# Banded attention woven into a four-block feed-forward: token copies, the pace of the attention pairs, and the order of a few steps

## The chip, the cores and the metric

The kernel runs on 1 core of one Trainium2 chip. The time is device microseconds of one execution. Two executions of the kernel before gave 535.16 and 535.59 us, a median of 535.38 us; the execution that was profiled took 535.26 us.

## The reference

An attention with a banded mask feeds a bilinear feed-forward:

```
scores = q @ k^T / 8 + bias(head, key distance)    # 4 batches, 8 heads, 768 tokens, 64 per head
keep   = key < 8  or  0 <= query - key < 96
x      = softmax(scores where kept) @ v            # as a 3072 x 512 matrix of tokens
out    = ((x @ w1) * (x @ w2)) @ w3 @ w_out        # 512 -> 1024 -> 1024 -> 512, all float32
```

Since at most 104 keys are kept for a query, the kernel computes scores only in bands of 136 columns.

## The kernel before, in words

**Attention.** The 3072 tokens are 24 blocks `s` of 128 queries; two blocks make a pair `d` (0 to 11) of 256 tokens. A block goes through `scores` (L762, TensorE), `maxima` (L776, VectorE adds the bias and takes the row maximum, per quarter `q` and head half), `exponentials` (L785, ScalarE), `sums` (L792), `scale_part` (L809) and `turn` (L814), the last three on VectorE: they normalise and transpose the weights. When both blocks of a pair are turned, `values` (L822, TensorE) multiplies with `v` in 192 small matmuls, the first 64 of which need only the pair's first block, and `tokens` (L902) copies the result out of PSUM on ScalarE. One PSUM tile `sc` holds scores and values in turn.

**Feed-forward.** Tokens are taken in units `u`: unit 1 holds pairs 2 and 3 and multiplies plainly ("U", `first`, L278: half a product is six 512-column matmuls). Units 2 and 3 hold four blocks of 256 tokens each and use the seven-product scheme of fast matrix multiplication (`Sevenths`): for each of eight chunks `f` of the 1024 hidden columns come products p = 1, 5, 4 (of the chunk before), 6, 2, 3 (of the chunk before), 7, each of six matmuls, accumulated in two PSUM tiles `x` and `y`. After each, `take` (L400) works on the sums: p = 1, 6, 5 are copied by ScalarE (L410), p = 2, 7, 4, 3 are added or multiplied by VectorE (L412 to L419). p = 1 opens a tile (`room`, L394) in a ring of three buffers, tag `ag`, which output tiles also use. Unit 4 (`Wide`, L432) does the same on 512-token blocks made from pairs 8 to 11. "Z" items (`third`, L312) are the second multiplication, three 512-column matmuls with the folded matrix `w3 @ w_out`, eight for each 128 tokens.

**Operands.** All operands are split in a high and a low part (ScalarE copies, VectorE subtracts). The weights `w12h` and `w12l` hold eight chunks; while unit 1 multiplies, VectorE and ScalarE form sums of weight blocks (`join` L201, `combine` L209, `sums_high`, `sums_low`) and write them out to DRAM; `bring` (L243) loads them back into the first seven eighths of the same buffers for units 2 to 4. The last eighth then is free. The tokens of pairs 8 and 9 wait there: `wide_tokens` (L858) copies them from PSUM into a tile of the `ag` ring, and two DMAs per pair move them on (L866). Later `first_tokens` and `first_low` (L939, L949) split them, and `next_tokens` (L957) makes the other operands of unit 4 in seven steps, placed at the Z items of unit 3 that `WIDE_AT` (L57) names.

**Order.** Until pair 4 the order is written out (`ORDER`). From there `planned` (L997) lists the feed-forward's items, and a loop places attention steps between them: `on(k)` (L1105) emits the next k items, `rows` (L1108) emits the quarters of a block with the given number of items after each, `rest` (L1116) emits `sums`, `scale_part` and `turn` in one or two parts, with an item between parts. Per pair `MEET` (L59) has the item before which `values` stands, the one before which the next pair's `scores` stand, and the paces of its two blocks: SLOW is two items after each quarter, QUICK is 1, 2, 1, 2. Every engine runs its instructions in that order, and DMAs are issued from SP in that order too. For pairs 4 and 5 the loop has its own paces.

Of the kernel before, what the change touches and what calls it, by code (L numbers as in the profile page):

```python
# [20 lines left out]
P = 128  # L21
# [70 lines left out]
class FeedForward:  # L92
# [3 lines left out]
    def __init__(self, ctx, tc, w12, w3k, w3t, w_out, out):  # L96
        self.nc = tc.nc
        self.w12, self.w3k, self.w3t, self.w_out, self.out = w12, w3k, w3t, w_out, out
        self.wp = wp = ctx.enter_context(tc.tile_pool(name="wp", bufs=1))
        self.mp = ctx.enter_context(tc.tile_pool(name="mp", bufs=2))  # L100
        self.ps = ctx.enter_context(tc.tile_pool(name="ps_m", bufs=4, space=PSUM))
        self.w = [wp.tile([P, NFC, 2, NCC, P], F32R, name=f"w12{x}") for x in "hl"]
        self.wh, self.wl = wp.tile([P, NFC, DO], F32R, name="wh"), [None] * NFC
        self.places, self.free, self.raw = list(range(NFC)), [NFC], {}

        self.wo = self.mp.tile([P, NFC, DO], I32, tag="gh", bufs=1, name="wo")
        gl = self.mp.tile([P, 2, 4 * PC], I32, tag="gl", bufs=1, name="stage")
# [4 lines left out]
        self.wf = [w.rearrange("p f n i m -> p (f n i m)") for w in self.w]  # L112

# [80 lines left out]
    def high(self, f):  # L194
        self.nc.scalar.activation(self.w[0][:, f].rearrange("p n i m -> p (n i m)"), self.t3s[:, f % 2].bitcast(F32), AF.Copy)

    def low(self, f):
        hi, lo = (w[:, f].rearrange("p n i m -> p (n i m)") for w in self.w)
        self.nc.vector.tensor_tensor(out=lo, in0=self.t3s[:, f % 2].bitcast(F32), in1=hi.bitcast(F32), op=ALU.subtract)

    def join(self, f):  # L201

        if f == 0:
            self.sums = self.xp.tile([P, 2, 4, 2 * P], F32, tag="xh", name="block_sums")
            self.parts = self.xp.tile([P, 2, 4, 2 * P], F32R, tag="xl", name="block_parts")
        hi, lo = (w[:, f].rearrange("p n i m -> p (n i m)").bitcast(F32) for w in self.w)
        self.nc.vector.tensor_tensor(out=self.sums[:, f % 2].rearrange("p k m -> p (k m)"), in0=hi, in1=lo, op=ALU.add)
# [19 lines left out]
    def blocks_out(self, f):  # L227
        for h in range(2):
            x = self.w[h][:, f].bitcast(F32).rearrange("p n (k i) m -> p n k (i m)", k=2)
# [3 lines left out]
    def restore(self):  # L233
        for f in range(NFC):
            for h in range(2):
                x = self.w[h][:, f].bitcast(F32).rearrange("p n (k i) m -> p n k (i m)", k=2)
                self.nc.sync.dma_start(out=x[:, 0], in_=self.ws[f, :, 0:2, h])
                self.nc.sync.dma_start(out=x[:, 1], in_=self.ws[f, :, 3:6:2, h])
# [30 lines left out]
class Unit:  # L269
# [8 lines left out]
    def first(self, f, n, half):  # L278

        if half == 0:  # L280
            self.ps[f, n] = self.ff.ps.tile([P, self.width], F32, tag="m", name=f"m_{self.c}_{f}_{n}")
        ps, (xh, xl) = self.ps[f, n], self.x
        for i in range(half * NCC // 2, (half + 1) * NCC // 2):
            mh, ml = (w[:, f, n, i] for w in self.ff.w)
# [78 lines left out]
class Sevenths(Unit):  # L363
# [36 lines left out]
    def take(self, p, f):  # L400
# [6 lines left out]
        y, z = (self.bank(k, f)[0] if p != 1 else None for k in (5, 2))  # L407
# [231 lines left out]
def banded(ctx, tc, ff, ns, nt, n1, nf, oki, qk, vx, sc, pr):  # L639
# [218 lines left out]
    def wide_tokens(d):  # L858

        x = d % 2 * T  # L860
        if d // 2 == LAST:
            raw = ff.mp.tile([P, NCC, T], F32, tag="ag", bufs=3, name=f"tokens_{d}")
            nc.scalar.activation(raw, sc[:, :, :T], AF.Copy)
            for k in range(2):
                to = ff.wf[k][:, 2 * SLOT:].bitcast(F32).rearrange("p (i t) -> p i t", i=2)
                nc.sync.dma_start(out=to[:, :, x:x + T], in_=raw[:, 2 * k:2 * k + 2])  # L866
            return
# [6 lines left out]
        b11, b21 = (ff.wf[k][:, 2 * SLOT:] for k in range(2))  # L874
# [12 lines left out]
        def hi(to, x):  # L887
            return lambda: nc.scalar.activation(to, x, AF.Copy)

        later[LAST] = [  # L890
# [5 lines left out]
            [sub(b11, b22, b22h)],  # L896
            [sub(b21, raw, t4h)],
        ]
        view = dict(b11=(a[:, :n], a[:, n:]), b21=(b[:, :n], b[:, n:]), t1=(t1h, t1l), t2=(t2h, t2l), t3=(t3h, t3l), t4=(t4h, b21), b22=(b22h, b11))
# [39 lines left out]
    def first_tokens(u, k=0):  # L939

        if u == LAST:
            if k == 0:
                homes[u] = [xp.tile([P, 2048], F32R, tag="xh", name=f"xh{i}_{u}") for i in range(2)]
            nc.scalar.activation(homes[u][k][:, :1024], ff.wf[k][:, 2 * SLOT:].bitcast(F32), AF.Copy)
            return
        homes[u] = [xp.tile([P, 2048], F32R, tag=tag, name=f"{tag}0_{u}") for tag in ("xh", "xl")]
        nc.scalar.activation(homes[u][0][:, :1024], ff.tokens[:, 0], AF.Copy)

    def first_low(u, k=0):  # L949

        if u == LAST:
            x = homes[u][k]
            nc.vector.tensor_tensor(out=x[:, 1024:], in0=ff.wf[k][:, 2 * SLOT:].bitcast(F32), in1=x[:, :1024].bitcast(F32), op=ALU.subtract)
# [21 lines left out]
    units, homes, later = {}, {}, {}  # L975
# [21 lines left out]
    def planned():  # L997
# [43 lines left out]
        for u in range(1, last + 1):  # L1041
# [11 lines left out]
            for t in range((2 if u < last else 4) * T // P):  # L1053
                for j, f in enumerate(line(u)):
# [23 lines left out]
                    if t == 3 and 0 <= j < 5 and u < last:  # L1078
                        yield seventh(u + 1, 0, (1, 5, 6, 2, 7)[j])

    with tc.manual_schedule(engines={mybir.EngineType.PE}):
        with tc.manual_schedule(engines={mybir.EngineType.DVE, mybir.EngineType.SP, mybir.EngineType.Activation, mybir.EngineType.Pool}):
            ordered()
        with tc.manual_schedule(engines={mybir.EngineType.Activation, mybir.EngineType.DVE}):
# [42 lines left out]
            for d in range(STEPS // 2, PAIRED):  # L1127
# [16 lines left out]
            for d in range(PAIRED, n // 2):  # L1144
# [3 lines left out]
                for s in (2 * d, 2 * d + 1):  # L1148
                    rows(s, MEET[d][2 + s % 2])
                    if s % 2 == 0:  # L1150
# [4 lines left out]
                    on(1)  # L1155
                    rest(s, 2)
# [51 lines left out]
```

## Time and profile before

| | |
|---|---|
| profiled execution | 535.26 us, span of its instructions 533.5 us |
| TensorE (PE) busy | 507.2 us, 95% of the span |
| VectorE (DVE) busy | 348.3 us, 65% |
| ScalarE (ACT) busy | 228.1 us, 43% |
| mean granted TensorE clock | 0.984 of full |

PE is busy nearly throughout, so the span is its work plus the places in which it waits, plus what it does at a lower clock. A row of a timeline has the start, the length, the engine, the line, the operation with the tiles it writes and reads, and in brackets how long the engine had been idle before it, with what ended the idle time. A matmul's length contains its pipeline latency: the next one starts before it ends.

### The profile page before, as it was taken

Reading aid. Unit: us, or ns where it says so; the run is one execution under the profiler, and the core shown is the slowest. Engines: PE = TensorE matmul, PEld = TensorE weight load, DVE = VectorE, ACT = ScalarE, POOL = GpSimd, SP = SyncE. Lnnn points to the kernel's source line nnn. Section 1 sums busy time; section 2 is a strip of 40 time slices with the busy share of each in tenths; the row PEclk is TensorE's granted clock in tenths of the full one; section 3 lists DMA queues with packets and bytes.
Section 4 is the critical chain, followed back from the end, with each engine's and each line's share of the span. In section 5 each row is a group of like instructions: output and inputs, shape, how many; then the busy total and the mean of one; then the engine's idle time right before and its main releaser. Section 6 shows DMA issues by size and latency. Waiting matters only on the chain. (4 is left out here: it accounts for less than half of the span.)

```text
span 533.5 us, 13891 instructions
## 1 busy us (share of the span) xinstructions
PE 507.2 (95%) x5812; PEld 409.0 (77%) x5812; DVE 348.3 (65%) x878; ACT 228.1 (43%) x662; POOL 4.0 (1%) x29
## 2 busy tenths in 40 slices
PE   7999999999999599998999999699989999999997
PEld 5445478888888488888998878699868888887885
DVE  7999888998988916677686575386773333336110
ACT  7157856354453323554545454455533121222220
POOL 2000000000000000000000000000000000000000
PEclk9999999999999889999999999799989999999999
DMA  8998629993699966378914266781011573100111
GB/s 317 418 342 340 268 81 304 363 355 105 211 318 307 301 218 212 127 238 271 346 65 119 88 236 214 260 283 62 2 40 62 162 215 117 38 1 6 54 41 63
DMA packets 40087, 100.97 MB, mean 189 GB/s; under 512 B 3538, under 2 KB 22994, under 8 KB 38482
## 3 DMA queue, kind: packets, MB, share of 16 engines
q1 hardware_dynamic: 39872, 99.76, 54.3%
q8 instruction: 47, 0.77, 0.6%
q10 hardware_dynamic: 146, 0.26, 0.1%
q14 instruction: 22, 0.18, 0.1%
HBM read 75.89 MB, written 23.07 MB: 186 GB/s over the span
## 5 line engine op out<-in xcount | busy, mean ns | idle before, releaser
L790 ACT ACTIVATE pr<-pr,mx 128x136 f32<-128x136 f32 (+2 forms) x192 | 74.8, 392 | 41.5 <-DVE mx L783 41.4
L410 ACT ACTIVATE ag<-x 128x256 f32<-128x256 f32 (+1 forms) x48 | 21.7, 452 | 79.2 <-PE x L385 70.6
L318 PE MATMUL o<-wh,gh 128*128 128x512 f32 x128 | 51.5, 402 | 0.1
L285 PE MATMUL m<-xh,w12h 128*128 128x512 f32 x128 | 50.2, 392 | 0.0
L319 PE MATMUL o<-wl,gh 128*128 128x512 f32 x128 | 50.1, 392 | 0.0
L320 PE MATMUL o<-wh,gl 128*128 128x512 f32 x128 | 50.1, 391 | 0.0
L286 PE MATMUL m<-xl,w12h 128*128 128x512 f32 x128 | 49.8, 389 | 0.0
L287 PE MATMUL m<-xh,w12l 128*128 128x512 f32 x128 | 49.8, 389 | 0.0
L834 PE MATMUL sc<-pt,vr 32*64 32x160 f32 (+4 forms) x2112 | 35.7, 279 | 8.6 <-DVE pt L820 8.6
L834 PEld LDWEIGHTS sc<-pt,vr 32*64 32x64 f32 x2112 | 32.9, 138 | 14.3 <-DVE pt L820 10.5
L385 PE MATMUL x<-xh,w12h 128*128 128x256 f32 (+1 forms) x152 | 34.9, 309 | 6.9 <-ACT ag L410 5.2
L820 DVE STREAM_TRANSPOSE pt<-pr 128x640 f32<-128x640 f32 (+1 forms) x36 | 37.5, 1055 | 2.1 <-ACT pr L805 1.8
L790 ACT ACTIVATION_READ_ACCUMULATOR pr<-pr,mx 128x1 f32 x192 | 36.4, 189 | 0.0
L783 DVE CUSTOM_DVE_ANT_0 pr<-sc,biasw 128x136 f32<-128x136 f32 x144 | 34.3, 294 | 2.1 <-PE sc L774 1.9
L385 PE MATMUL x<-xh,w12l 128*128 128x256 f32 (+1 forms) x152 | 34.1, 304 | 1.3 <-ACT ag L410 0.7
L385 PEld LDWEIGHTS x<-xh,w12h 128*128 128x128 f32 x152 | 26.9, 195 | 9.4 <-ACT ag L410 5.6
L336 ACT ACTIVATE ot<-o 128x512 f32<-128x512 f32 x23 | 13.6, 593 | 39.1 <-PE o L320 39.0
L252 PE MATMUL w<-wo,kt 128*128 128x512 f32 x64 | 28.5, 599 | 1.8 <-DVE wo L188 1.1
L385 PE MATMUL x<-xl,w12h 128*128 128x256 f32 (+1 forms) x96 | 29.6, 322 | 0.0
L385 PE MATMUL x<-xl,w12l 128*128 128x256 f32 (+1 forms) x96 | 29.2, 318 | 0.0
L385 PEld LDWEIGHTS x<-xh,w12l 128*128 128x128 f32 x152 | 26.2, 190 | 3.8 <-ACT ag L410 1.2
L318 PEld LDWEIGHTS o<-wh,gh 128*128 128x128 f32 x128 | 24.3, 190 | 5.9 <-issue 1.3
(195 smaller groups left out, 1066.2 us busy)
## 6 DMA issues: line engine op xcount, KB each, us to landing
qr<-qk SPq DMA_DIRECT2D x20, 720.0 KB, 6.9
w12h<-ws SPq DMA_DIRECT2D x16, 512.0 KB, 4.8
w12l<-ws SPq DMA_DIRECT2D x16, 512.0 KB, 5.1
vr<-vx SPq DMA_DIRECT2D x8, 768.0 KB, 6.3
w12h<-ws SPq DMA_DIRECT2D x8, 768.0 KB, 5.7
w12l<-ws SPq DMA_DIRECT2D x8, 768.0 KB, 6.1
out_dram<-ot SPq DMA_DIRECT2D x23, 256.0 KB, 2.1
raws<-w SPq DMA_DIRECT2D x5, 1024.0 KB, 6.0
```

The lines of the kernel that those rows point to most:

```text
L252: self.nc.tensor.matmul(self.prod[f], lhsT=block.bitcast(F32), rhs=self.wo[:, k].bitcast(F32), start=k == 0, stop=k == NFC - 1)
L285: self.nc.tensor.matmul(ps, lhsT=mh, rhs=xh[:, i], start=i == 0, stop=False)
L286: self.nc.tensor.matmul(ps, lhsT=mh, rhs=xl[:, i], start=False, stop=False)
L287: self.nc.tensor.matmul(ps, lhsT=ml, rhs=xh[:, i], start=False, stop=i == NCC - 1)
L318: self.nc.tensor.matmul(ps, lhsT=gh, rhs=ff.wh[:, f], start=f == first, stop=False)
L319: self.nc.tensor.matmul(ps, lhsT=gh, rhs=ff.wl[f], start=False, stop=False)
L320: self.nc.tensor.matmul(ps, lhsT=gl, rhs=ff.wh[:, f], start=False, stop=f == last)
L385: self.nc.tensor.matmul(out, lhsT=w[:, i], rhs=x[:, i], start=fresh and i == 0 and j == 0, stop=i == 1 and j == 2, skip_group_check=True)
L783: nc.vector.tensor_tensor_reduce(out=pr[:, q, u, GLB + w0:GLB + w1], in0=scored(s, u, q, w0, w1), in1=bias, scale=-SCALE, scalar=3.0e38, o ...
L790: nc.scalar.activation(x, x, AF.Exp, bias=mx[:, q, u:u + 1], scale=-1.0, accum_out=sm[:, q, u:u + 1])
L820: nc.vector.transpose(strided(pts[d][:, (half * NR + q0) * 2 * PF:], [PF, 2 * (q1 - q0)], [P, NR + 1], [1, R]), x.rearrange("p n (k c) -> ...
L834: nc.tensor.matmul(sc[cols, hp, n0 * R:n1 * R], lhsT=v[rows, i, cols], rhs=turned, start=i == i0, stop=i == NV - 1, skip_group_check=True)
```

## The change

- **Copies.** The eighth chunk of the weights gets two buffers of its own (`tail0`, `tail1`). Pairs 8 and 9 are copied by ScalarE straight from PSUM into them, in two instructions of 128x512 instead of one of 128x1024; the `ag` tile and the four DMAs are gone. The low parts of two operands of unit 4 are later written into the same buffers.
- **Pair 4.** Its second block has one item after each quarter instead of two, and no four items behind them; its first block is scaled and turned in halves. Its `values` stand after 19 items of unit 1 instead of 21.
- **Pairs 6 to 11.** The items before which `values` stand (24, 53, 80, 105, 134, 161) become 28, 58, 86, 112, 142, 169: four items more for pair 6, one more for each of pairs 7 to 10, none for pair 11. Behind the last `turn` of a pair, `values` follow after 3, 2, 2, 2, 2 and 1 items, where it was 1 for all. In pairs 7 to 11 the second block's `scores`, and in pairs 6 to 10 the load of later keys, move from before the first block's `sums` to between its `scale_part` and `turn`, three items later.
- **Unit 4.** The seven steps stand four to seven Z items later; its first products come in the order 1, 2, 5, 6, 7; in its last chunks, the split of chunks 4 to 6 stands after product 4 of the last chunk instead of product 3 of the one before.

```diff
-SPLITS = {(7, 6): (0, 4), (6, 3): (4, 7), (7, 3): (7, 8)}
-WIDE_AT = (1, 5), (1, 6), (1, 7), (2, 1), (2, 2), (2, 4), (2, 6)
+SPLITS = {(7, 6): (0, 4), (7, 4): (4, 7), (7, 3): (7, 8)}
+WIDE_AT = (2, 4), (2, 5), (2, 6), (2, 7), (3, 0), (3, 1), (3, 2)
-MEET = {6: (24, 27, QUICK, SLOW), 7: (53, 56, SLOW, SLOW), 8: (80, 83, SLOW, QUICK), 9: (105, 108, QUICK, QUICK), 10: (134, 137, SLOW, SLOW), 11: (161, 0, SLOW, QUICK)}
+MEET = {6: (28, 31, SLOW, SLOW), 7: (58, 61, SLOW, SLOW), 8: (86, 89, SLOW, QUICK), 9: (112, 115, QUICK, QUICK), 10: (142, 145, SLOW, SLOW), 11: (169, 0, SLOW, QUICK)}
...
-        self.w = [wp.tile([P, NFC, 2, NCC, P], F32R, name=f"w12{x}") for x in "hl"]
+        self.w = [wp.tile([P, NFC - 1, 2, NCC, P], F32R, name=f"w12{x}") for x in "hl"]
+        self.ends = self.last_blocks()
...
+    def tail(self, k, name, dtype):
+        return self.wp.tile([P, 2 * NCC * P], dtype, tag=f"tail{k}", name=f"{name}{k}")
...
         if d // 2 == LAST:
-            raw = ff.mp.tile([P, NCC, T], F32, tag="ag", bufs=3, name=f"tokens_{d}")
-            nc.scalar.activation(raw, sc[:, :, :T], AF.Copy)
+            if d % 2 == 0:
+                raws.extend(ff.tail(k, "raw", F32) for k in range(2))
             for k in range(2):
-                to = ff.wf[k][:, 2 * SLOT:].bitcast(F32).rearrange("p (i t) -> p i t", i=2)
-                nc.sync.dma_start(out=to[:, :, x:x + T], in_=raw[:, 2 * k:2 * k + 2])
+                to = raws[k].rearrange("p (i t) -> p i t", i=2)
+                nc.scalar.activation(to[:, :, x:x + T], sc[:, 2 * k:2 * k + 2, :T], AF.Copy)
             return
...
+        def last_low(k):
+            def do():
+                x = ff.tail(k, "tail_low", F32R)
+                sub(x, *((b22, b22h), (raw, t4h))[k])()
+                units[LAST].blocks[("b22", "t4")[k]][1] = x.rearrange("p (i t) -> p i t", i=2)
+            return do
...
-            [sub(b11, b22, b22h)],
-            [sub(b21, raw, t4h)],
+            [last_low(1)],
+            [last_low(0)],
...
-                        yield seventh(u + 1, 0, (1, 5, 6, 2, 7)[j])
+                        yield seventh(u + 1, 0, ((1, 5, 6, 2, 7) if u < last - 1 else (1, 2, 5, 6, 7))[j])
...
-            def rest(s, parts):
+            def rest(s, parts, between=None):
                 sums(s)
                 cuts = [(k * NR // parts, (k + 1) * NR // parts) for k in range(parts)]
                 for step in (scale_part, turn):
+                    if step == turn and between:
+                        between()
                     for q0, q1 in cuts:
...
-                for s, every in zip((2 * d, 2 * d + 1), (1, 1) if d % 2 else (1, 2)):
-                    rows(s, (every,) * NR)
-                    on(4 if every == 2 else 3 - s % 2 * 3)
-                    rest(s, 1)
+                for s in (2 * d, 2 * d + 1):
+                    rows(s, (1,) * NR)
+                    first = d % 2 == 0 and s % 2 == 0
+                    on(2 if first else 0 if s % 2 else 3)
+                    rest(s, 2 if first else 1)
                     if s % 2 == 0:
-                        on(2)
+                        on(1 if first else 2)
...
                     rows(s, MEET[d][2 + s % 2])
-                    if s % 2 == 0:
+                    on(1)
+
+                    def middle():
                         if d > PAIRED:
                             scores(s + 1)
                         if d < n // 2 - 1:
                             keys(s + 3)
-                    on(1)
-                    rest(s, 2)
+
+                    rest(s, 2, middle if s % 2 == 0 else None)
```

## Rows read from the trace of the kernel before

**Rows 1.** Page, the granted TensorE clock in 40 slices of 13.3 us, in tenths

```profile
PEclk9999999999999889999999999799989999999999
```

**Rows 2.** Waits of PE: us in total, how many, the longest

```profile
PE sc L834 <- DVE pt L820: 8.6, 3, 5.8
PE x L385 <- ACT ag L410: 5.9, 3, 4.7
PE x L385 <- DVE ag L414: 2.2, 3, 0.8
...
PE sc L774 <- DVE mx L783: 0.9, 1, 0.9
```

**Rows 3.** Timeline of PE, pair 4: first and last of 126 matmuls, then its values

```profile
151.24 0.50 PE L285 MATMUL m<-xh,w12h 128*128 128x512 f32 x1
...
179.71 0.39 PE L287 MATMUL m<-xh,w12l 128*128 128x512 f32 x1
180.02 1.02 PE L834 MATMUL sc<-pt,vr 32*64 32x32 f32 x64
186.79 3.56 PE L834 MATMUL sc<-pt,vr 32*64 32x160 f32 x128 [5.75 <-DVE pt L820]
```

**Rows 4.** Groups of DVE instructions, 166 to 187 us: busy us, mean ns | idle before

```profile
L213 DVE TENSOR_TENSOR block_sums<-block_sums 128x256 f32<-128x256 f32 x12 | 5.1, 422 | 0.3
L220 DVE TENSOR_TENSOR block_sums<-block_sums,block_parts 128x1024 fp32r<-128x1024 f32 x3 | 3.6, 1206 | 0.0
...
L305 DVE TENSOR_TENSOR gl<-ag,gh 128x512 fp32r<-128x512 f32 x4 | 2.7, 685 | 0.0
L295 DVE TENSOR_TENSOR ag<-m,ag 128x512 f32<-128x512 f32 x4 | 2.7, 677 | 0.0
L207 DVE TENSOR_TENSOR block_sums<-w12h,w12l 128x1024 f32<-128x1024 f32 x2 | 2.4, 1223 | 1.0 <-DMA ws<-block_sums 1.0
```

**Rows 5.** Timeline of DVE: the last transposition of pair 4

```profile
185.23 1.51 DVE L820 STREAM_TRANSPOSE pt<-pr 128x1280 f32<-128x1280 f32 x1
```

**Rows 6.** Busy time by stretch: length, PE, PEld, DVE, ACT, POOL (instructions), granted clock, DMA

```profile
183.40:190.20 6.80, 3.40 (x128) 3.41 (x128) 4.34 (x6) 0.69 (x1) 0.00 (x0) 0.51 0.78 263
336.90:343.80 6.90, 4.61 (x22) 4.61 (x23) 3.55 (x20) 3.91 (x16) 0.00 (x0) 0.51 0.61 239
391.40:394.60 3.20, 3.08 (x99) 2.79 (x83) 0.11 (x1) 1.02 (x1) 0.00 (x0) 0.50 0.03 5
```

**Rows 7.** Timelines of SP, ACT and PE around 339 us; landing times of the token copies

```profile
331.91 0.61 SPq L866 DMA_DIRECT2D w12l<-tokens  x1
...
338.76 0.38 ACT L410 ACTIVATE ag<-x 128x256 f32<-128x256 f32 x1 [7.53 <-DMA w12l<-tokens]
...
339.19 0.58 PE L385 MATMUL x<-xh,w12h 128*128 128x256 f32 x1 [4.71 <-ACT ag L410]
...
DMA to landing us min/median/max: 5.3/6.1/6.7
```

**Rows 8.** Page, the costliest groups: ScalarE's copies of 128x512 out of PSUM

```profile
L336 ACT ACTIVATE ot<-o 128x512 f32<-128x512 f32 x23 | 13.6, 593 | 39.1 <-PE o L320 39.0
```

**Rows 9.** Timelines of DVE and PE, pair 11

```profile
386.61 1.23 DVE L953 TENSOR_TENSOR xh<-w12l,xh 128x1024 fp32r<-128x1024 f32 x1 [1.21 <-ACT xh L944]
...
390.35 3.04 PE L834 MATMUL sc<-pt,vr 32*64 32x160 f32 x128 [2.33 <-DVE pt L820]
```

**Rows 10.** Timelines of DVE and PE, unit 4's last chunks

```profile
483.03 0.95 DVE L465 TENSOR_TENSOR xlg<-g,xhg 128x768 fp32r<-128x768 f32 x1
...
484.64 0.50 PE L385 MATMUL x<-t4h,w12l 128*128 128x512 f32 x1 [0.84 <-DVE pr L414]
```

**Rows 11.** Timeline of DVE, block 19: its first maximum and its transposition

```profile
320.31 0.29 DVE L783 CUSTOM_DVE_ANT_0 pr<-sc,biasw 128x136 f32<-128x136 f32 x1
...
326.81 1.57 DVE L820 STREAM_TRANSPOSE pt<-pr 128x640 f32<-128x640 f32 x2
```

**Rows 12.** Timeline of DVE: the last of the seven steps for unit 4

```profile
404.12 1.23 DVE L885 TENSOR_TENSOR w12l<-sums,t4h 128x1024 fp32r<-128x1024 f32 x1
```

More of the change, by code (lines that the diff above doesn't have):

```diff
@@ L112, in __init__, with last_blocks, block @@
         self.wf = [w.rearrange("p f n i m -> p (f n i m)") for w in self.w]
+    def tail(self, k, name, dtype):
+        return self.wp.tile([P, 2 * NCC * P], dtype, tag=f"tail{k}", name=f"{name}{k}")
+    def last_blocks(self):
+        return [self.tail(k, "w12e", F32R).rearrange("p (n i m) -> p n i m", n=2, i=NCC) for k in range(2)]
+    def block(self, f):
+        return [w[:, f] for w in self.w] if f < NFC - 1 else self.ends
     def more_stages(self, xp, bp):
@@ L194, in high @@
     def high(self, f):
-        self.nc.scalar.activation(self.w[0][:, f].rearrange("p n i m -> p (n i m)"), self.t3s[:, f % 2].bitcast(F32), AF.Copy)
+        self.nc.scalar.activation(self.block(f)[0].rearrange("p n i m -> p (n i m)"), self.t3s[:, f % 2].bitcast(F32), AF.Copy)
     def low(self, f):
-        hi, lo = (w[:, f].rearrange("p n i m -> p (n i m)") for w in self.w)
+        hi, lo = (w.rearrange("p n i m -> p (n i m)") for w in self.block(f))
         self.nc.vector.tensor_tensor(out=lo, in0=self.t3s[:, f % 2].bitcast(F32), in1=hi.bitcast(F32), op=ALU.subtract)
@@ L205, in join @@
             self.parts = self.xp.tile([P, 2, 4, 2 * P], F32R, tag="xl", name="block_parts")
-        hi, lo = (w[:, f].rearrange("p n i m -> p (n i m)").bitcast(F32) for w in self.w)
+        hi, lo = (w.rearrange("p n i m -> p (n i m)").bitcast(F32) for w in self.block(f))
         self.nc.vector.tensor_tensor(out=self.sums[:, f % 2].rearrange("p k m -> p (k m)"), in0=hi, in1=lo, op=ALU.add)
@@ L228, in blocks_out @@
         for h in range(2):
-            x = self.w[h][:, f].bitcast(F32).rearrange("p n (k i) m -> p n k (i m)", k=2)
+            x = self.block(f)[h].bitcast(F32).rearrange("p n (k i) m -> p n k (i m)", k=2)
             self.nc.sync.dma_start(out=self.ws[f, :, 0:2, h], in_=x[:, 0])
@@ L233, in restore @@
     def restore(self):
+        self.ends = self.last_blocks()
         for f in range(NFC):
             for h in range(2):
-                x = self.w[h][:, f].bitcast(F32).rearrange("p n (k i) m -> p n k (i m)", k=2)
+                x = self.block(f)[h].bitcast(F32).rearrange("p n (k i) m -> p n k (i m)", k=2)
                 self.nc.sync.dma_start(out=x[:, 0], in_=self.ws[f, :, 0:2, h])
@@ L283, in first @@
         for i in range(half * NCC // 2, (half + 1) * NCC // 2):
-            mh, ml = (w[:, f, n, i] for w in self.ff.w)
+            mh, ml = (w[:, n, i] for w in self.ff.block(f))
             self.nc.tensor.matmul(ps, lhsT=mh, rhs=xh[:, i], start=i == 0, stop=False)
@@ L406, in take @@
         x = self.bank(1, f)[0]
-        y, z = (self.bank(k, f)[0] if p != 1 else None for k in (5, 2))
+        y, z = (self.bank(k, f)[0] if p in users else None for k, users in ((5, (5, 3)), (2, (2,))))
         g = [self.g[f][:, k * self.half:(k + 1) * self.half] for k in range(2)]
@@ L873, in wide_tokens @@
         b12, b22 = (both[:, k * n:(k + 1) * n] for k in range(2))
-        b11, b21 = (ff.wf[k][:, 2 * SLOT:] for k in range(2))
+        b11, b21 = raws
         homes[LAST] += [xp.tile([P, 2 * n], F32R, tag="xl", name=f"xl{k}_{LAST}") for k in range(2)]
@@ L895, in wide_tokens @@
             [sub(t2l, raw, t2h), sub(raw, b21, raw), hi(t4h, raw)],
-            [sub(b11, b22, b22h)],
-            [sub(b21, raw, t4h)],
+            [last_low(1)],
+            [last_low(0)],
         ]
-        view = dict(b11=(a[:, :n], a[:, n:]), b21=(b[:, :n], b[:, n:]), t1=(t1h, t1l), t2=(t2h, t2l), t3=(t3h, t3l), t4=(t4h, b21), b22=(b22h, b11))
+        view = dict(b11=(a[:, :n], a[:, n:]), b21=(b[:, :n], b[:, n:]), t1=(t1h, t1l), t2=(t2h, t2l), t3=(t3h, t3l), t4=(t4h, t4h), b22=(b22h, b22h))
         units[LAST] = Wide(ff, LAST, {k: [x.rearrange("p (i t) -> p i t", i=2) for x in y] for k, y in view.items()}, 2 * LAST * T, xp, sc, pr)
@@ L943, in first_tokens @@
                 homes[u] = [xp.tile([P, 2048], F32R, tag="xh", name=f"xh{i}_{u}") for i in range(2)]
-            nc.scalar.activation(homes[u][k][:, :1024], ff.wf[k][:, 2 * SLOT:].bitcast(F32), AF.Copy)
+            nc.scalar.activation(homes[u][k][:, :1024], raws[k], AF.Copy)
             return
@@ L952, in first_low @@
             x = homes[u][k]
-            nc.vector.tensor_tensor(out=x[:, 1024:], in0=ff.wf[k][:, 2 * SLOT:].bitcast(F32), in1=x[:, :1024].bitcast(F32), op=ALU.subtract)
+            nc.vector.tensor_tensor(out=x[:, 1024:], in0=raws[k], in1=x[:, :1024].bitcast(F32), op=ALU.subtract)
             return
@@ L973, in sizes @@
         warm(0)
-    units, homes, later = {}, {}, {}
+    units, homes, later, raws = {}, {}, {}, []
     do = dict(pj=ff.join, bo=ff.blocks_out, ps=ff.combine, sh=ff.sums_high, sl=ff.sums_low, so=ff.sums_out, A=lambda *x: ff.convert(0, *x), B=lambda *x: ff.convert(1, *x), C=lambda *x: ff.convert(2, *x), wh=ff.high, wl=ff.low, F=ff.fold, pe=ff.fold_out, ph=ff.fold_high, pl=ff.fold_low, S=scores, R=maxima, E=exponentials, s=sums, c=lambda s: scale(s, nc.scalar if s < FIRST else nc.vector), X=turn, V=values, h=high, l=low, bias=distances, bD=masks, bE=globals_near, biasA=biases, nt=sizes)
```

## The prediction, made before the changed kernel ran

> **What bounds the kernel now.** I read the clock by slice first, then PE's waits, then the timelines around the longest of them. PE is the engine on which the end depends: it is busy 507 of 533.5 us, and the clock is full except in three places [rows 1]. So time can be won only where PE waits or runs slowly. In PE's waits [rows 2] two kinds make up most: `values` waiting for a transposition (8.6 us in three waits) and product 6 waiting for ScalarE's copy (5.9 in three). The rest are waits below 1 us. The timelines place the big ones: 5.75 us in pair 4 [rows 3], 4.71 us near 339 us [rows 7] and 2.33 us in pair 11 [rows 9]. The three stretches at the lower of the two levels (0.50 to 0.51, that is 1.2 GHz) begin in or right after these waits and last 3 to 7 us [rows 6]. So each long wait is paid for twice: once as idle time, once as slow work behind it.
>
> **A, pair 4: 7.4 us.** PE has the first 64 matmuls of `values` done at 181.04 and then stands until 186.79 [rows 3], when DVE ends the transposition of the second block [rows 5]. DVE has hardly a pause in that time: it is simply behind, since the four items with two products after each quarter, and the four items after them, put weight sums ahead of the transposition. With the new pace the items 14 and later come behind it. From the code these hold, of the groups in [rows 4]: 8 of the 12 L213 (3.4 us), one L207 (1.2, and the 1.0 that it waits for a DMA), one L220 (1.2), two L295 and two L305 (2.7). Together 9.5 us; I take 8.5, since DVE's neighbours overlap a little. The transposition would end near 186.7 - 8.5 = 178.2. PE's 126 matmuls up to `values` took 28.8 us, 0.226 each [rows 3]; 19 items instead of 21 end 2.7 us earlier, at 177.3, and with the first 64 small matmuls PE asks for the second half at 178.3. So the wait goes, or a few tenths of it stay. Splitting the first block's scaling and turning adds two DVE starts, a tenth or two, which the same slack holds. With the wait goes the slow stretch: 3.40 us of work at 0.51 lose 3.40 x 0.49 = 1.7. A = 5.75 + 1.7 = 7.4. Lower bound: DVE is 2 us later than I count, and 3.5 remain of it to win.
>
> What is late next? The sums moved back (some 9 us) run while PE is in `values` and the next items; product 3 of unit 1 is the one that PE needs first, three items after `values`, some 6 us after the transposition, and it is second in DVE's line. Covered.
>
> **B, the token copies: 7.0 us.** The wait at 339.19 is product 6 behind a copy by ACT, and that copy waited 7.53 us for a DMA [rows 7]: `room` got the `ag` buffer that pair 9's token tile held until its second DMA had landed, 6 us after 331.91. No tile, no DMA, no wait: the ring's third buffer then last held an output tile, whose DMA is issued long before. Idle 4.71, and 4.61 us of work at 0.51 lose 2.3 [rows 6]: B = 7.0. What is added: two copies of 128x512 at 0.59 [rows 8] instead of one of 128x1024, between nothing and 0.6 us more on ACT per pair; three products stand between them and the next `scores`, so 0. The four DMA issues leave SP's queue and nothing is behind them that PE had been waiting for: 0. The seven steps' last two results go to the same memory as before: 0.
>
> **C, pair 11: 3.9 us.** Here DVE is late because first_low for unit 4 stands in the middle of block 23 and itself waits 1.21 us for ACT [rows 9]. Eight items later, block 23 starts at the Z items of the second row tile, and the first_low work falls into block 22's steps. From block 23's `scores` to the second half of `values` PE then has 13 Z items of three matmuls (13 x 0.68 = 8.8) and the first 64 small ones (1.0): 9.9 us. Block 19's chain from first maximum to last transposition took 328.38 - 320.31 = 8.1 [rows 11], and at most two items (1.4) come ahead of it: 9.5. It just fits. Idle 2.33, and 3.08 us at 0.50 lose 1.5: C = 3.9, at worst 0 if the first_low work pushes block 23 back by another 2 us.
>
> **D, unit 4: 0.8 us.** The 0.84 us wait is product 4 behind a DVE addition, and the 0.95 us split stood right ahead of that [rows 10]. Moved behind, it meets Z item 4 two products later: covered.
>
> **E, other waits: 1.4 us.** The 0.9 us of `scores` behind maxima goes [rows 2], for `scores` now come when all maxima of the block before are done. Of the first kind 8.6 - 5.75 - 2.33 = 0.5 is pair 6, which gets two more items behind its last turn. The small waits for L414 and L410 (2.2 and 5.9 - 4.71 = 1.2) I leave as they are: the pace of pairs 7 to 11 is only one item per pair slower. They may vanish (3.4 more) or double (3.4 less).
>
> **F, added: 0.3 us.** In unit 4's first chunk products 6 and 7 now have one Z item (0.68) between them, and ACT's copy of 512 columns takes 0.59 [rows 8] plus a start: 0 to 0.5, I take 0.3. The seven steps ended 12.0 us after `values` of pair 11 did (405.35 against 393.39, [rows 12, 9]); in the new order PE reaches the product that needs them after 13 Z items and 7 products of twice their length, 18 us: 0. Keys loaded three items later still have a pair's length until use: 0.
>
> **Sum.** A + B + C + D + E - F = 7.4 + 7.0 + 3.9 + 0.8 + 1.4 - 0.3 = 20.2. From the profiled execution's 535.26, 0.1 us below the median, that gives 515.
>
> The Trainium skill, "TensorE: Matmul & The Clock Gate", Terms, prices a throttled clock as throttled time x (1 - K/N), which is half of it here. By that rule the three stretches [rows 6], 16.9 us long, would cost 8.5, not the 5.5 that I count, and the sum would come to 512. The rows speak against it: in 5.7 of those us PE had no matmul to slow, and that time is in the waits already.
>
> **Rivals.**
> 1. *One large wait stays* (A or B or C, each for its own reason: DVE further behind, the `ag` buffer held by the output tile's DMA, block 23 pushed back), or the small waits double and one more comes. 4 to 7 us less: 519 to 523. For it: C fits by 0.4 us only. Against it: A and B have named causes that the change takes away. Chance 0.20.
> 2. *The gain is given back.* PE no longer pauses, so DVE and ACT lose the pauses in which they caught up, and each of pairs 5 to 11 gets a wait of 1 to 2 us that [rows 2] does not show: 7 x 1.5 = 10, about 526. For it: DVE needs 348 of the 533 us and all of the attention lies in the first 400. Against: pairs 7 and 8 ran at nearly the same pace, and no wait of 1 us stands there. Chance 0.10.
> 3. *Slower: the moved `scores`.* DVE's queue is in order, and a block's maxima stand ahead of the takes that PE needs. From the second block's `scores` to `values` there were 16 to 18 items in pairs 7 to 11; now there are 13 to 16. If the chain of 8.1 us [rows 11] doesn't fit and each of these five pairs pays what pair 4 paid (7.4), the time is 535.3 - 7.4 - 7.0 - 0.8 + 4 x 7.4 + 3.5 = 553. It decides from 6.0 us per pair (29.8 in all for 546). Against: even 14 items are 9.5 us and 1.0 more, longer than chain and start. Chance 0.04. The same page of the Trainium skill (Architectural detail) calls ACT and DVE strict FIFO; DVE's order here agrees, and by that rule such a wait would hold back the takes as well.
> 4. *All small waits go as well*: 511 to 512. Chance 0.06.
>
> **Numbers.** The forecast, 515 with its own 512 to 518, has 0.60. Range 509 to 524: it takes in rivals 1 and 4. About 2% is what can be told from no change, 524.7 or less being faster. Faster takes the forecast, rivals 1 and 4: 0.86 less a little of rival 1's upper end, 0.84. Same: rival 2 and that end, 0.12. Slower 0.04.
>
> **What would show it.** Right: PE's `values` in pair 4 run without a wait for the transposition; no ACT copy waits for a DMA; the clock is full in every slice; PE's waits fall by some 15 us. Wrong: PE waits of over 2 us for DVE pt or ACT ag, above all in pairs 7 to 11, or PE waiting for weights from DRAM, which it never did before.

## The result, and the profile after

The changed kernel takes 518.15 us (median of 2 executions, 517.68 to 518.62) against 535.38 (535.16 to 535.59): a ratio of 0.9678, 95% interval 0.9637 to 0.972. It is faster, and 3 us above the forecast of 515. The profiled execution took 517.68 us, with a span of 515.9.

First the clock by slice (page). It is full in all 40 slices; the three dips of [rows 1] are gone.

```profile
PEclk9999999999999999999999999999999999999999
```

Then all waits of PE (us in total, how many, the longest).

```profile
PE sc L845 <- issue: 3.5, 3, 1.6
PE sc L785 <- issue: 1.5, 1, 1.5
PE w L263 <- DVE wo L198: 1.5, 1, 1.5
PE x L396 <- DVE ag L425: 1.4, 2, 0.8
PE warmed L675 <- DVE warm L671: 1.1, 1, 1.1
PE w L263 <- DVE kt L198: 0.8, 1, 0.8
PE y L396 <- ACT ag L421: 0.4, 1, 0.4
PE o L329 <- issue: 0.2, 1, 0.2
```

Against [rows 2], `values` (now L845) no longer waits for a transposition, nor product 6 for ScalarE's copy. The sum fell from 22.4 to 10.4 us. But half of these 10.4 is new: waits that end with "issue", that is, with no releaser the profile knows.

The two large removals, in the order of [rows 3, 5, 7]. Pair 4's last transposition (timeline of DVE) and its `values` (timeline of PE):

```profile
175.25 1.51 DVE L831 STREAM_TRANSPOSE pt<-pr 128x1280 f32<-128x1280 f32 x1
```

```profile
177.15 2.82 PE L845 MATMUL sc<-pt,vr 32*64 32x32 f32 x192
```

The transposition ends at 176.76 instead of 186.74, before PE begins, and all 192 matmuls stand in one row without a bracket. The copies of pair 9's tokens and the next products' copies (timeline of ACT):

```profile
327.09 1.09 ACT L877 ACTIVATE raw<-sc 128x512 f32<-128x512 f32 x2 [3.97 <-PE sc L845]
328.65 0.39 ACT L421 ACTIVATE ag<-x 128x256 f32<-128x256 f32 x1 [0.47 <-PE x L396]
...
335.06 0.39 ACT L421 ACTIVATE ag<-x 128x256 f32<-128x256 f32 x1 [0.99 <-PE x L396]
```

Every copy now waits for PE's product, none for a DMA. Pair 11, where [rows 9] had 2.33 us of waiting (timeline of PE):

```profile
378.82 2.99 PE L845 MATMUL sc<-pt,vr 32*64 32x32 f32 x192
```

And what is new, in the same view: the scores of pair 7's first block (L785) and the values of pairs 8 and 10 (L845).

```profile
247.88 0.42 PE L785 MATMUL sc<-qr 64*32 64x136 f32 x5
249.80 1.15 PE L785 MATMUL sc<-qr 64*32 64x136 f32 x59 [1.50 <-issue]
...
297.74 2.79 PE L845 MATMUL sc<-pt,vr 32*64 32x32 f32 x188
302.15 0.30 PE L845 MATMUL sc<-pt,vr 32*64 32x32 f32 x4 [1.62 <-issue]
...
351.67 2.66 PE L845 MATMUL sc<-pt,vr 32*64 32x32 f32 x174
355.85 0.41 PE L845 MATMUL sc<-pt,vr 32*64 32x64 f32 x18 [1.53 <-issue]
```

PE stops in the middle of a burst: 4, 18 or 59 matmuls before its end. The operands are there: the matmuls on both sides of a stop read the same tiles, and pair 8's last transposition ended at 297.10. A fourth such wait, of 0.37 us, is in the values of pair 9.

**What these waits are.** PE's instructions can be counted up to each wait. Busy time of each engine to 300.31 us, where the last matmul ahead of the second long wait starts (instructions in brackets: PE, PEld, DVE, ACT, POOL; then granted clock, DMA share and GB/s):

```profile
0.00:300.31 300.31, 294.82 (x3912) 228.84 (x3912) 245.82 (x636) 154.66 (x474) 3.87 (x29) 1.00 0.73 254
```

3912 matmuls and 3912 weight loads, with 49 other instructions of PE's queue in the trace, make 7873; counted from 0, the next one has the index 7873, and the wait is ahead of it. Counted so for all four:

```
burst                      index of the instruction that waits     starts of PE wait this long apart (us)
scores, pair 7             6081 = 23 x 256 + 193                    1.78
values, pair 8             7873 = 30 x 256 + 193                    1.84
values, pair 9             8641 = 33 x 256 + 193                    0.59
values, pair 10            9665 = 37 x 256 + 193                    1.74
```

All lie at 193 over a multiple of 256. The DMA queues (packets, MB, share of 16 engines) have one that fits, q8; first the whole page, then 298 to 300.6 us, ahead of the wait of pair 8, then 300.6 to 302.1 us, in it, where the view has no q8 at all:

```profile
q8 instruction: 47, 0.77, 0.6%
```

```profile
q8 instruction: 1, 0.02, 3.3%
```

```profile
q1 hardware_dynamic: 8, 0.01, 3.6%
```

47 packets of 16 KB for some 11,700 instructions of PE are about one packet for 256 instructions, 64 bytes each. The one ahead of pair 8's wait travels from 299.20 to 300.56 us, and PE, which stops at 300.53, goes on at 302.15, 1.59 us after the packet has ended. In the other three waits PE goes on 1.62, 1.33 and 1.35 us after such an end, and by number these packets are the 23rd, 30th, 33rd and 37th of q8, the factors of 256 in the table. So I read the waits as PE waiting for the next block of its own program. In a burst of `values` 384 instructions go by in 2.8 us, 7.3 ns each, and 256 of them in 1.9; among the long products a block lasts up to 29 us. The Trainium skill, "Runtime: NRT & Kernel Launch", Instruction fetch mechanics, has the same blocks of 16 KiB and 256 instructions, and calls the cost of crossing one "mostly hidden". The blocks agree with these rows; "mostly" holds for 41 of 45 ends, and the other four cost 5.0 us.

### The profile page after: what moved, and what is told of

The parts are those of the page before. It is cut to its first block, busy times and chain, and to the rows that moved or that the text cites. A ratio compares the mean times of both kernels' runs of the same rounds, so it can differ in the third digit from the quotient of the medians.

```text
span 515.9 us, 13902 instructions
## 1 busy us (share of the span) xinstructions
PE 501.3 (97%) x5812; PEld 404.1 (78%) x5812; DVE 348.3 (68%) x880; ACT 229.0 (44%) x664; POOL 3.9 (1%) x29
## 5 line engine op out<-in xcount | busy, mean ns | idle before, releaser
L296 PE MATMUL m<-xh,w12h 128*128 128x512 f32 x112 | 43.9, 392 | 0.0
L298 PE MATMUL m<-xh,w12l 128*128 128x512 f32 x112 | 43.6, 389 | 0.0
L297 PE MATMUL m<-xl,w12h 128*128 128x512 f32 x112 | 43.6, 389 | 0.0
L845 PEld LDWEIGHTS sc<-pt,vr 32*64 32x64 f32 x2112 | 30.9, 130 | 8.3 <-issue 5.4
L845 PE MATMUL sc<-pt,vr 32*64 32x160 f32 (+4 forms) x2112 | 32.9, 266 | 3.5 <-issue 3.5
L396 PE MATMUL x<-xh,w12h 128*128 128x256 f32 (+1 forms) x152 | 33.5, 302 | 0.8 <-DVE ag L425 0.8
L263 PE MATMUL w<-wo,t 128*128 128x512 f32 x64 | 28.4, 597 | 0.0
```

What stands on the lines that cost most here:

```text
L263: self.nc.tensor.matmul(self.prod[f], lhsT=block.bitcast(F32), rhs=self.wo[:, k].bitcast(F32), start=k == 0, stop=k == NFC - 1)
L396: self.nc.tensor.matmul(out, lhsT=w[:, i], rhs=x[:, i], start=fresh and i == 0 and j == 0, stop=i == 1 and j == 2, skip_group_check=True)
L845: nc.tensor.matmul(sc[cols, hp, n0 * R:n1 * R], lhsT=v[rows, i, cols], rhs=turned, start=i == i0, stop=i == NV - 1, skip_group_check=True)
```

## The experiments

Medians, and ratios to runs of the kernel before on the same chip. "No releaser" is the sum of PE's waits on "issue" in the profiled execution, added up from the rounded lines of the view. The kernel before had medians of 537.04, 537.03, 537.21 and 536.64 us in the four groups. All runs but pair4_old are faster than it by more than 2%; the interval of pair4_old reaches above 0.98.

| run | median us | ratio, 95% interval | span profiled | no releaser |
|---|---|---|---|---|
| group 1: pair4_old | 527.91 | 0.9824 (0.9777 to 0.9871) | 527.5 | 5.3 |
| copies_old | 523.06 | 0.9738 (0.9694 to 0.9782) | 524.2 | 5.1 |
| pace_old | 522.42 | 0.9736 (0.9696 to 0.9775) | 519.8 | 0.2 |
| scores_early | 520.28 | 0.9677 (0.963 to 0.9724) | 518.5 | 5.2 |
| group 2: after_again | 517.46 | 0.9643 (0.9616 to 0.9669) | 517.4 | 4.5 |
| shift_64 | 524.27 | 0.976 (0.9732 to 0.9788) | 521.0 | 7.6 |
| values_parted | 517.02 | 0.963 (0.9603 to 0.9658) | 515.2 | 3.1 |
| group 3: warm_plus_20 | 519.99 | 0.9677 (0.9642 to 0.9713) | 517.6 | 5.2 |
| parted_plus_20 | 518.03 | 0.9648 (0.9615 to 0.9681) | 516.0 | 2.6 |
| group 4: parted_8_10 | 516.43 | 0.963 (0.9596 to 0.9664) | 514.0 | 0.6 |
| after_third | 516.92 | 0.9642 (0.9609 to 0.9674) | 514.6 | 3.8 |

Theory 1 is that the new waits are ends of instruction blocks that the new order has put into bursts of small matmuls; the rival, that they belong to the new pace or its data. The first four runs undo one part of the change each and try steps A to F at the same time.

**pair4_old**, the changed kernel with pair 4's old pace:

```diff
-for s in (2 * d, 2 * d + 1):
-    rows(s, (1,) * NR)
-    first = d % 2 == 0 and s % 2 == 0
-    on(2 if first else 0 if s % 2 else 3)
-    rest(s, 2 if first else 1)
+for s, every in zip((2 * d, 2 * d + 1), (1, 1) if d % 2 else (1, 2)):
+    rows(s, (every,) * NR)
+    on(4 if every == 2 else 3 - s % 2 * 3)
+    rest(s, 1)
     if s % 2 == 0:
-        on(1 if first else 2)
+        on(2)
```

> The changed kernel with pair 4's old pace (two products after each quarter of its second block, four behind them, scaling and turning in one part, values after 21 products). If the queue order of DVE made pair 4's wait, PE stands again some 5.8 us before the second half of pair 4's values, at half clock for some us behind it, and the time is 518.2 + 7.4 = 525 to 526. Rival: the wait was removed by something else in the change, or it is made up for later, because PE's standing gives other engines and PE's instruction supply time to run ahead: 518 to 521.

Its timeline of PE, and the busy time of PE, PEld, DVE, ACT and POOL around this wait and behind the values of pair 9, with the granted clock:

```profile
180.50 1.02 PE L845 MATMUL sc<-pt,vr 32*64 32x32 f32 x64
187.47 3.68 PE L845 MATMUL sc<-pt,vr 32*64 32x160 f32 x128 [5.95 <-DVE pt L831]
```

```profile
185.20:192.10 6.90, 4.63 (x130) 4.38 (x131) 3.29 (x3) 0.90 (x1) 0.00 (x0) 0.51 0.69 241
338.50:343.00 4.50, 4.50 (x81) 4.05 (x80) 1.12 (x2) 1.95 (x5) 0.00 (x0) 0.62 0.89 325
```

The wait is back, 5.95 us, and 4.63 us of work at 0.51 lose 2.3: 8.2 in the trace, where A said 7.4. The time is 527.91, above the 525 to 526 expected. By the medians the difference to after_again is 10.4 (527.91 - 517.46, the kernel before being equal in both groups), by the spans 10.1 (527.5 - 517.4). The rest is in the values of pair 9: their wait without a releaser is 1.5 us here and 0.4 in after_again, and 4.50 us of work at 0.62 behind it lose another 1.7, where after_again has no slow stretch.

**copies_old**, tokens of pairs 8 and 9 through the `ag` tile and four DMAs again:

```diff
+raw = ff.mp.tile([P, NCC, T], F32, tag="ag", bufs=3, name=f"tokens_{d}")
+nc.scalar.activation(raw, sc[:, :, :T], AF.Copy)
 for k in range(2):
     to = raws[k].rearrange("p (i t) -> p i t", i=2)
-    nc.scalar.activation(to[:, :, x:x + T], sc[:, 2 * k:2 * k + 2, :T], AF.Copy)
+    nc.sync.dma_start(out=to[:, :, x:x + T], in_=raw[:, 2 * k:2 * k + 2])
```

> The changed kernel with the tokens of pairs 8 and 9 copied through a tile of the ag ring and two DMAs per pair, as before, into the new buffers. If the ring made the wait, an ACT copy of product 1 waits again several us for a copy's DMA, PE behind it, and the clock falls: 518.2 + 7.0 = 525. Rival: with values of pair 9 seven products later the ring's tile falls where a room is not asked for within 6 us, and the wait is under 2 us and costs no clock: 518 to 520.

Timeline of PE, and the 7 us behind the wait:

```profile
337.81 0.58 PE L396 MATMUL x<-xh,w12h 128*128 128x256 f32 x1 [4.59 <-ACT ag L421]
```

```profile
338.00:345.00 7.00, 7.00 (x40) 7.00 (x41) 4.47 (x22) 4.18 (x18) 0.00 (x0) 0.63 0.71 261
```

4.59 idle, and 7.0 us at 0.63 lose 2.6: 7.2, where B said 7.0; the profiled spans differ by 6.8 (524.2 against 517.4), the medians by 5.6. The time, 523.06, is 2 us below the 525 expected.

**pace_old**, the old `MEET`, place of the scores and of the key loads, `WIDE_AT`, `SPLITS` and first products of unit 4:

```diff
-MEET = {6: (28, 31, SLOW, SLOW), 7: (58, 61, SLOW, SLOW), ..., 11: (169, 0, SLOW, QUICK)}
+MEET = {6: (24, 27, QUICK, SLOW), 7: (53, 56, SLOW, SLOW), ..., 11: (161, 0, SLOW, QUICK)}
...
-on(1)
...
-rest(s, 2, middle if s % 2 == 0 else None)
+if s % 2 == 0:
+    middle()
+on(1)
+rest(s, 2)
```

> The changed kernel with the old paces of pairs 6 to 11, scores and key loads in their old place, the old places of unit 4's seven steps, its old first order and the old split. What is left of the change is pair 4 and the copies. Three waits of PE that name no releaser (1.5 to 1.6 us each, in the middle of scores of pair 7, values of pair 8 and values of pair 10) are new in the changed kernel. Theory 1: they come from blocks of 256 PE instructions that end inside a burst of small matmuls; the old pace puts the bursts elsewhere in the instruction stream, so these waits go (5.3 us), while pair 11's wait with its slow stretch (3.9), the 0.8 us of the split and the 1.4 us of other waits come back: 518 to 520. Theory 2: they come with the two large waits that are gone (PE and its suppliers lost the pauses), whatever the pace: then they stay, and all 6.1 us come on top: 524.

PE's waits:

```profile
PE sc L845 <- DVE pt L831: 2.9, 2, 2.3
PE x L396 <- DVE ag L425: 2.2, 3, 0.8
PE x L396 <- ACT ag L421: 1.3, 2, 0.8
...
PE sc L785 <- DVE mx L794: 0.9, 1, 0.9
PE x L396 <- DVE pr L425: 0.8, 1, 0.8
```

Pair 11's wait (2.3), unit 4's (L425 pr, 0.8) and all the small ones of [rows 2] are back, and the waits inside bursts are gone. So C, D and E are the work of this part, and so are the new waits. The median, 522.42, is 5.0 us above after_again and lies between the two that I had given for it, 518 to 520 and 524: theory 1 has the waits right and the time 2 us too low.

**scores_early** puts only the scores and the key loads back, in front of the first block's `sums` (the second half of the diff above).

> The changed kernel with the second block's scores and the key load back in front of the first block's sums; all else as changed. By the prediction the 0.9 us wait of scores behind maxima comes back and perhaps a second one like it: 518.5 to 520. Rival: moving the scores shortened the second block's time and costs something that is hidden among the small waits; then the time falls by 1 us or more.

0.9677 against 0.9643 can't be told apart, the intervals overlap. The 0.9 us wait of the scores behind maxima, which I had expected back, did not come. So the other paces are enough to remove it, and the move, to which step E had put it down, is not needed for that. The price of rival 3, scores that come too late, does not show either.

**after_again** is the changed kernel, as a reference in its group.

> The changed kernel unaltered, for a comparison on the same chip and a second profile. 517.5 to 518.7. The three waits without a releaser stand at the same matmuls if they depend on the place in PE's instruction stream (instruction 6081, 7873 and 9665, each 193 above a multiple of 256); if they come from chance meetings with DMA traffic alone, one or two are elsewhere.

The waits stand at the same four indices, 6081, 7873, 8641 and 9665, with 1.3, 1.6, 0.4 and 1.0 us.

**shift_64** issues 32 warming products fewer at the start, so that all later instructions of PE have an index 64 lower.

```diff
-WARM = (24, 42)
+WARM = (24, 10)
```

> The changed kernel with 32 warming matmuls fewer at the start, 64 PE instructions, so that all later bursts of small matmuls lie 64 instructions earlier in the stream. Theory 1, blocks of 256 instructions: the waits in values of pair 8 and pair 10 go, since a block no longer ends in the last third of these bursts; bursts in which a block then ends in their last third are those of pair 5 and pair 11, and waits of 1 to 1.6 us appear there. The sum stays: 517 to 519, with up to 1 us more if the start suffers. Theory 2, a wait for data or a buffer that the profile does not show: the waits stay in values of pair 8 and pair 10, after the same matmuls.

The timeline of PE has the waits in new places: values of pairs 1, 2 and 5 (and 11, 0.68 us, not shown), and the scores that follow pair 1.

```profile
72.79 0.42 PE L845 MATMUL sc<-pt,vr 32*64 32x64 f32 x19 [1.02 <-issue]
...
79.08 0.67 PE L785 MATMUL sc<-qr 64*32 64x136 f32 x25 [1.35 <-issue]
...
126.86 0.44 PE L845 MATMUL sc<-pt,vr 32*64 32x64 f32 x26 [0.85 <-issue]
...
224.46 0.35 PE L845 MATMUL sc<-pt,vr 32*64 32x64 f32 x17 [1.87 <-issue]
...
305.87 2.82 PE L845 MATMUL sc<-pt,vr 32*64 32x32 f32 x192
```

Pair 8 runs through (305.87), and so does pair 10. The instructions that wait have the indices 1473, 1729, 2497, 5057, 6081, 8641 (0.5 us, among products) and 10433: again all 193 over a multiple of 256, mostly other multiples. Pairs 1 and 2 don't even stand in a part of the program that the change touches. That settles it against the rival: the waits go with the index. But they are more than I had expected, which was pairs 5 and 11 alone and a time of 517 to 519; it is 524.27. The profiled spans differ by 3.6 us (521.0 against 517.4), of which 3.1 are waits without a releaser (7.6 against 4.5). The start lost nothing: PE waits 3.1 us for the first weights instead of 1.4, since it has less to do until then, and its first product with them starts at 7.72 us, in after_again at 8.33. Why the medians differ by 6.8 is open.

**values_parted** gives the same work in shorter bursts: `values` of pairs 6 to 11 in two parts.

```diff
+go(start + MEET[d][0] - 2)
+values(d, 0, NR)
 go(start + MEET[d][0])
-values(d)
+values(d, NR)
```

> The changed kernel with the values of pairs 6 to 11 in two parts, the first block's 64 (or 16) matmuls two products ahead of the rest (for pair 11 one). Theory 1: a block of 256 instructions then takes 1.4 us longer wherever it lies in such a burst, so the waits of 1.5 to 1.6 us shrink to a few tenths: 515 to 516. Theory 2: the waits stay as they are, 518.

Pair 8 in its timeline, and pair 9:

```profile
296.40 1.02 PE L845 MATMUL sc<-pt,vr 32*64 32x32 f32 x64
298.95 2.12 PE L845 MATMUL sc<-pt,vr 32*64 32x160 f32 x128
...
327.07 0.44 PE L845 MATMUL sc<-pt,vr 32*64 32x64 f32 x25 [1.95 <-issue]
```

Pairs 8 and 10 have no wait any more; pair 9's rose from 0.4 to 1.95, since an end of a block now falls into its first part, 3.7 us of running ahead of the next one. 4.5 became 3.1 us; the time (517.02 against 517.46) shows no difference, and the 515 to 516 of theory 1 did not come.

**warm_plus_20** and **parted_plus_20** try the index again, by 40 upwards: 62 warming products instead of 42, in the changed kernel and in values_parted.

> The changed kernel with 62 instead of 42 warming products at the start, so that every later TensorE instruction has an index 40 higher. They run 3.67 to about 7.1 us, inside the wait for the first weight tile, and cost nothing. Theory 1 (waits stand where a block of 256 instructions ends, at index 193 over a multiple of 256, and only where that falls among small matmuls): the wait of the scores of pair 6 (index 6081) goes, since the block now ends among the long products 20 instructions ahead of them; those of values 8 and 10 fall 40 instructions earlier in their bursts, where the second block of the burst still ends inside it: pair 8 keeps about 1.1 us, pair 10 half a us to none. Waits without a releaser 5.2 -> 1.5 to 2.5 us, time 515 to 516. Rival (they belong to the changed pace and its data, wherever the blocks end): all three stay, 5 us in sum, and the time stays at 517 to 518.

> As values_parted (values of pairs 6 to 11 in two parts, two items apart) and 62 warming products as well. There two waits without a releaser were left, of 1.9 us in the values of pair 9 (index 8641) and 1.0 in the scores of pair 6 (index 6081). Theory 1: with all instructions 40 later, the first of these blocks ends 40 instructions earlier, but the block before it now ends ahead of the first part of the values of pair 9, among long products, some us earlier, so that this wait goes or falls under 0.5; the second block ends ahead of the scores, so that its wait goes; no other burst has two ends closer together than 3.4 us. Waits without a releaser under 1 us in all, span 512 to 514, time 513 to 515: faster than both kernels. Rival (the waits belong to the pace): 2.9 us stay, time 516 to 518.

Most of this was wrong. Pair 9's wait went, pair 8 kept about 1 us in the first, and pairs 8 and 10 none in the second, as expected; but pair 10 kept 1.2 us in the first, and both times are 3 to 5 us above those given. In sum the waits came out as the rival had them (5.2 where it had 5, and 2.6 where it had 2.9); against it speak the places alone. The end at 6081, which should have been harmless among the products ahead of the scores, costs more there than in the scores (timelines of PE, warm_plus_20, then parted_plus_20):

```profile
249.16 0.38 PE L396 MATMUL x<-xl,w12l 128*128 128x256 f32 x1 [2.56 <-issue]
```

```profile
248.83 0.58 PE L396 MATMUL x<-xl,w12l 128*128 128x256 f32 x1 [2.35 <-issue]
```

In both, as in the changed kernel, PE goes on at 248.8 to 249.8, 5.1 to 6.0 us after the end of the block before, which lies in the values of pair 6. Moving the index moved where PE stood, not until when. So theory 1 had to be said better: what counts is the time from one end to the next, whatever is done in it.

**parted_8_10** uses that: parts for pairs 8 and 10 alone, and the scores after pair 6 two items later, so that this block lasts longer by itself.

```diff
-MEET = {6: (28, 31, SLOW, SLOW), ...
+MEET = {6: (28, 33, SLOW, SLOW), ...
...
-go(start + MEET[d][0])
-values(d)
+if d in (8, 10):
+    go(start + MEET[d][0] - 2)
+    values(d, 0, NR)
+    go(start + MEET[d][0])
+    values(d, NR)
+else:
+    go(start + MEET[d][0])
+    values(d)
```

> The changed kernel with the values of pairs 8 and 10 alone in two parts, two items apart (in values_parted that took away both waits there), those of pair 9 in one burst as in the changed kernel, and the first scores of pair 7, which follow the values of pair 6, two items later (33 instead of 31). The block that ends at index 6081 came 5.1 to 6.0 us after the end of the block before it in every kernel with the new pace, beside transfers that kept the DMA engines 0.93 to 0.98 busy. Theory 1 (a block comes 3 to 6 us after the end of the one before it, and TensorE waits when it is through in less): with two more items of products ahead of the scores, the block lasts some 2 us longer by itself, so that the wait at 6081 goes or falls under 0.5; those at 7873 and 9665 go as in values_parted; that of pair 9 is 0.6 as in the changed kernel. Waits without a releaser 5.2 -> under 1.5 us, span 512 to 514, time 513.5 to 516, 2 to 3 us below the changed kernel run beside it. Rival (the waits move with the small matmuls and come back elsewhere, or the later scores make the maxima of pair 7 late): 3 us or more of waits, time as the changed kernel's.

> The changed kernel once more, beside parted_8_10: 517 to 518 us, with waits of 4.5 to 5.2 us without a releaser, ending at indices 6081, 7873, 8641 and 9665. Both theories expect the same of it.

after_third has the waits at the four indices expected, but 3.8 us of them, and a time just under the 517 to 518 expected (516.92).

PE's waits in parted_8_10:

```profile
PE w L263 <- DVE wo L198: 1.8, 1, 1.8
...
PE sc L845 <- DVE pt L831: 0.8, 1, 0.8
PE sc L845 <- issue: 0.4, 1, 0.4
PE x L396 <- ACT ag L421: 0.4, 1, 0.4
```

The waits fell from 3.8 in after_third to 0.6, each as expected. The time did not follow: 516.43, where 513.5 to 516 was expected, against 516.92; the ratios 0.963 and 0.9642 can't be told apart; the span is 514.0 against 514.6. Of the 3.2 us, 0.8 came back as a wait of pair 7's values for their transposition (its scores come later now), 0.4 behind a copy of ScalarE, and 0.6 at the start, which the edit doesn't touch. That leaves 1.4 expected and 0.6 measured in the profiled pair. It beats the kernel before; that it beats the changed kernel is not shown.

## Why the prediction was right, and where it was not

The terms of the forecast one by one: 20.2 us were predicted, the span fell by 17.6 (533.5 to 515.9).

- **A, B, C, D** (7.4 + 7.0 + 3.9 + 0.8 = 19.1): right in mechanism and place. The four waits and the three slow stretches are gone in the profile after. A's transposition was expected to end near 178.2 and ended at 176.76; PE was expected at 177.3 and came at 177.15. Undone alone, A costs 8.2 and B 7.2 in the trace (10.4 and 5.6 by the medians). The 5.5 us that these terms hold for the lower clock are borne out too: PE was busy for 507.2 us before and for 501.3 after (page), 5.9 less and not 8.5. C and D came back together in pace_old, with waits of 2.3 and 0.8.
- **E** (1.4): too small. I had left the waits for L414 and L410 as they were, 2.2 and 1.2 us, on the ground that one item more per pair changes little. All small waits but D's make 5.8 in the trace of before: 0.5 of pair 6, 0.9, 2.2 and 1.2, and 1.0 for `y` copies and output tiles, which [rows 2] leaves out. After has 1.8. So 4.0 went, 2.6 more than counted. The 0.9 us of scores behind maxima is among them, but it goes without the move of the scores as well (scores_early).
- **F** (0.3): nothing to be seen of it in PE's waits.
- **The sum** is the step that failed: it has no term for instruction blocks, and waits with no releaser cost 5.2 us, all but 0.2 of it at their ends. 19.1 + 4.0 - 5.2 = 17.9, against 17.6 measured; 0.3 are left open. (PE waits 0.4 us longer for the first weights, but its first product with them starts at 7.50 us, at 7.62 before.)

So two errors of opposite sign, +2.6 and -5.2, left the median 0.15 us above the forecast's own 512 to 518. That it came so near is in part luck: with E alone put right, the forecast would have been near rival 4 (511 to 512), and 5 to 6 us below the time measured. Rival 1 (a large wait stays) and rival 3 (late scores) did not happen. Rival 2 came true in part: gain was given back in waits that [rows 2] does not show, three of 1.5 to 1.6 us and one of 0.4, 5.0 us instead of seven and 10, though for another reason than a DVE or an ACT that falls behind. Of the signs of being right, three came true; the fourth, waits that fall by some 15 us, did not quite, for they fell by 12.0. The list of what would show me wrong named waits over 2 us for pt or ag, and weights from DRAM; a wait that names nobody was not on it. (Two small slips change no term: 28.8 / 126 is 0.228 and not 0.226, and 16.9 - 11.1 is 5.8 and not 5.7.) In the trace of before it could be foreseen only by counting: the ends of blocks lie at fixed indices, and moving `values` by a few items moves the burst over them.

## What to carry to other kernels

A wait in the middle of a burst that names no releaser is to be counted, not explained away: take the index of the instruction in its engine's queue, and if it repeats at one remainder of 256 and a packet of the instruction queue has ended shortly before the engine goes on (1.2 to 1.6 us here), it is the program that is late. Where several hundred instructions go by in some microseconds, longer work between two parts of the burst can remove the wait (it did in pairs 8 and 10, and made that of pair 9 longer), and any edit ahead of it, even of warming products at the start, can bring it back elsewhere. Nor is a wait that is gone a gain yet: parted_8_10 removed 3.2 us of them, and its time can't be told from that of the changed kernel. And a sum of removed waits should keep both a term for the small ones of the same cause and one for what the shorter order newly meets.

## What the runs showed of the hardware

- **Blocks of 256 instructions.** In all kernels here, every wait of PE over 0.3 us with no releaser, 39 in all, is at an index of 193 over a multiple of 256, and PE went on 1.2 to 1.6 us after the end of the packet of q8 that has the block's number. No block of any kernel began earlier than 1.0 us after that. The block that began so began 3.0 to 6.4 us after the one before it; no block that took over 4.7 us by itself was followed by such a wait. Blocks of 1.8 to 2.0 us did not always end in one: in an unparted burst of 384 instructions that two ends fall into, there was no wait where the first end came 3 to 29 instructions into the burst, and one of 0.9 to 2.2 us where it came 51 to 122 into it. In the first kind the packet travels before the burst begins (for pair 1 of the changed kernel from 64.29 to 65.37 us, the burst begins at 68.4); in the second it sets out 0.6 to 1.4 us after the first end. That the queue is read ahead of the engine by some tens of instructions, so that an early end is asked for before the burst begins, would explain it; no run here tried that. Where PE waited at 6081, the block came 5.1 to 6.4 us after the one before, those of pairs 8 and 10 3.1 to 4.1: the packet sets out 2.7 to 4.0 us after the end before, beside DMA engines that are busy throughout (a share of 0.97 to 1.02), and 0.7 to 1.4 us after it in pairs 8 and 10, beside idle ones. A full queue of transfers is not the whole reason, for in pair 9 it was as full and the packet set out after 1.3 to 1.7 us in most kernels.
- **The clock after such a wait.** The same wait of 1.6 us in pair 8 was followed by half the clock in after_again and not in the changed kernel's first profile. Length, busy time of PE, granted clock, DMA share and GB/s; after_again, then the changed kernel:

```profile
301.30:302.90 1.60, 0.05 (x2) 1.00 0.04 10
302.90:304.50 1.60, 1.60 (x8) 0.69 0.14 43
304.50:306.50 2.00, 2.00 (x6) 0.50 0.79 246
306.50:308.50 2.00, 2.00 (x69) 0.89 0.06 23
```

```profile
300.30:302.20 1.90, 0.28 (x24) 1.00 0.04 9
302.20:304.00 1.80, 1.80 (x11) 1.00 0.24 35
```

The first loses 1.6 x 0.31 + 2.0 x 0.50 + 2.0 x 0.11 = 1.7 us by it. One kernel's executions range over 3.0 us, 514.6 to 517.6 us of span at mean clocks of 0.995 to 1.000; one such stretch makes up to 1.7 of that. This is why differences below 3 us are left open here.
